# A Nyström attention fused with a feed-forward: all attention stages as tokens of one woven order

## The chip, the cores and the metric

The kernel runs on one core of one Trainium2 chip. The metric is the device time of one execution in microseconds (us). Engines are named as the profile does: PE is the matrix engine, PEld its weight loads, DVE the vector engine, ACT the activation engine, POOL the GpSimd engine and SP the engine that here only issues DMAs. PE, DVE, ACT and POOL each work through one instruction stream in order; so does each DMA-issuing queue (SP, ACT, POOL).

## The reference, cut to what matters

Batch 8, heads 8, sequence 576, head size 64, 32 landmarks. The output is `(A Z C v)` of each batch and head, laid out as tokens of 512 features, followed by a feed-forward.

```
q_lm, k_lm = means of 18 consecutive rows of q and of k          # 32 landmarks
A  = softmax(scale * q    k_lm^T)      # 576 x 32
Bm = softmax(scale * q_lm k_lm^T)      # 32 x 32
C  = softmax(scale * q_lm k^T)         # 32 x 576
Z  = Bm^T / (norm1(Bm) * norminf(Bm))
for _ in range(6): Z = 2 Z - Z Bm Z    # an approximate inverse
x  = (A Z C v)                         # rows of 512: heads side by side
out = (((x @ w1) * (x @ w2)) @ w3) @ w_out
```

## The kernel before, in words

**Folded weights.** `w3 @ w_out` is formed once (`fold`, L472), as 64 products of three matmuls each (L497) in split FP16, and kept as `w34`. Before it, tiles of w3 are transposed on PE (L484, "turn"), and both factors are split in a high and a low part by ACT and DVE (L477, L478, L489, L490). The products are a generator, and `steps(fd, n)` (L528) issues the next n of them, so that they fill PE while the first batch's attention is prepared.

**Attention of a batch.** The generator `attention` (L200) issues the stages of one batch, and each `yield` is a place where other work may be put in between. The eight heads are two quads of four heads. In order:

- scores C of a quad (`scores_c`, L205): twelve matmuls with 96 weight columns (a piece of transposed k), 64 moving columns each, into a `big` PSUM tile; an exp on ACT gives `ect` (L215). `presum` (L219) adds six parts of it on POOL to `es`, from which the column sums come.
- scores B, their exp and row sums, `bm` on POOL (L235 to L249); then its transposes and norms on DVE and POOL (L253 to L277).
- scores A (L283) with exp, and between the quads a product for the inverse's first residual (L303).
- context of a quad (`cv`, L313): 24 matmuls of C's exps with v (L317), followed by four small matmuls with a column of ones, one a head, for the sums (L322), a reciprocal and a scaled copy into `sz_`.
- six inverse steps (L376), each sixteen instructions on 32 x 32 array tiles, then two DVE evacuations (`tz_` L381, `sz_` L383) that the next step needs. Between them stand the row sums of A (`denominators`, L337), their reciprocals (L346) and the mix (L350, L352), which `normalise` (L357) spreads over partitions and multiplies into A.
- a closing product and `zt` (L398 to L404), then the product with the first-layer weights (L419), which gives `gt` ("widened" weights, evacuated by ACT L423 and DVE L425).

**Feed-forward of a batch.** `up` (L429) makes one 128-row piece of `x @ w1` or of `x @ w2` (named u and v below in the old order): four matmuls of 288 columns. The first kind is copied by ACT (L437), the second multiplied with it by DVE into `ab` (L439). There are 16 ups a batch. `down` (L446) multiplies 128 tokens of `ab` by `w34` in two halves of four matmuls with 512 columns (L451); after the second half ACT scales the sum into `o_sb` (L460), which is sent out.

**Loads.** q and k come in FP16 through POOL's queue; for batch 0 they are transposed on PE, for the others by DMA transposes on SP (`transposes`, L102; `turn_all` issues all four of a batch). `sums` (L171) adds the transposed rows to landmarks on POOL, with the DMA issues of a later batch's q and k in between; `landmarks` (L184) finishes them with a copy on ACT and an add on POOL. v comes in four pieces on SP, each after a one-element copy on ACT (L84).

**PSUM.** There are three `big` tiles (two banks each), one `small` and one `acc` tile.

**Order.** An opening (L548 to L624) loads weights, runs the fold and the attention of batch 0, in which the list of L605 says how many products go behind each attention step. The main loop (L646) then runs the ups of batch b while it steps through attention of batch b + 1. The order is a string of tokens, written out by hand, in which `a` is the next attention step:

```
MIXED = "u0 g a v0 u1 a v1 d u2 a v2 a d u3 v3 a s u4 v4 a p u5 d a v5 u6 a p v6 d a u7 p v7 a"
EVEN = "d a h p a h d a k d a d"
```

Of the kernel before, what the change touches and what calls it, by code (L numbers as in the profile page):

```python
# [31 lines left out]
def kernel(  # L32
# [11 lines left out]
    nc = tc.nc  # L44
    consts = ctx.enter_context(tc.tile_pool(name="consts", bufs=1))
# [55 lines left out]

    def transposes(st, t, hs):  # L102
        if "qkT" not in st:
            st["qkT"] = pat.tile([128, 2, H, 3, NP], FP16, name="qkT")
        n = len(hs)
        nc.sync.dma_start_transpose(
            out=st["qkT"][:, t, hs[0]:hs[0] + n, :, :].rearrange("p h c s -> p (h c) s"),
            in_=st["qkn"][0:NP, t, hs[0]:hs[0] + n, :].rearrange("p h f -> p (h f)"))


    def turn_on_pe(st, t, h0, copy):
        if "qkT" not in st:
            st["qkT"] = pat.tile([128, 2, H, 3, NP], FP16, name="qkT")
# [18 lines left out]
    def constants():  # L132
# [22 lines left out]
        nc.vector.memset(selc, 0.0)  # L155
        nc.vector.tensor_tensor(out=selr, in0=eye[:, 0, 0:8], in1=eye[:, 0, 8:16], op=ALU.add)
        nc.vector.reduce_sum(out=lomask, in_=eye[:, 0, 8:16], axis=AX.X)
        nc.vector.tensor_scalar(out=lomask, in0=lomask, scalar1=-1.0, scalar2=None, op0=ALU.mult)
        for c in range(4):
            sl = slice(32 * c, 32 * c + 32)  # L160
            for qd in range(2):
                nc.vector.tensor_copy(
# [4 lines left out]
        nc.vector.tensor_tensor(out=eye2, in0=eye, in1=eye, op=ALU.add)  # L167
# [32 lines left out]
    def attention(st, bank=None):  # L200
        bank = bank or small
        qkT, vt, qbd = st["qkT"], st["vt"], st["qbd"]
        ects = []

        def scores_c(qd):  # L205
            psC = big()
            pc = psC.rearrange("p a f -> p (a f)")
            for h in range(4):
                for c in range(3):
                    o = 64 * (3 * h + c)  # L210
                    nc.tensor.matmul(pc[0:NP, o:o + 64], qkT[:, 1, 4 * qd + h, c, :],  # L211
                                     qbd[:, 4 * qd + h, :, :].rearrange("p a m -> p (a m)"),
                                     start=True, stop=True)
            ect = pat.tile([128, 4, 6, 32], FP32, name="ect")
            nc.scalar.activation(out=ect[0:NP].rearrange("p h r m -> p (h r m)"),  # L215
                                 in_=pc[0:NP, 0:768], func=AXF.Exp, scale=SCALE / GRP)
            ects.append(ect)

        def presum(qd):  # L219
            e = ects[qd][0:NP]  # L220
# [3 lines left out]
            es = pz.tile([128, 4, 32], FP32, name="es")  # L224
# [3 lines left out]
            return es  # L228

        scores_c(0)  # L230
        es0 = presum(0)
        yield

        lm = st["lm"]
        psB = small()  # L235
        for qd in range(2):
            for h in range(4):
                nc.tensor.matmul(psB[32 * h:32 * h + 32, 32 * qd:32 * qd + 32],
                                 qbd[0:64, 4 * qd + h, 0, :], lm[0:64, 4 * qd + h, :],
                                 start=True, stop=True, tile_position=(0, 32 * h))  # L240
        ebm = pz.tile([128, 2, 32], FP32, name="ebm")
        nc.scalar.activation(out=ebm, in_=psB[:, 0:64].rearrange("p (a m) -> p a m", m=32),
                             func=AXF.Exp, scale=SCALE / (GRP * GRP))
        rbs = pz.tile([128, 2], FP32, name="rbs")
        nc.vector.reduce_sum(out=rbs, in_=ebm, axis=AX.X)
        nc.vector.reciprocal(out=rbs, in_=rbs)
        bm = pz.tile([128, 2, 32], FP32, name="bm")
        nc.gpsimd.tensor_tensor(out=bm, in0=ebm,
                                in1=rbs.unsqueeze(2).to_broadcast([128, 2, 32]), op=ALU.mult)  # L249
        yield  # L250

        scores_c(1)
        bt = pz.tile([128, 2, 32], FP32, name="bt")  # L253
        nc.vector.transpose(out=bt, in_=bm)
        btm = pz.tile([128, 2, 2, 32], FP32, name="btm")
        nc.gpsimd.tensor_tensor(
            out=btm, in0=bt.unsqueeze(2).to_broadcast([128, 2, 2, 32]),
            in1=par32.unsqueeze(1).unsqueeze(3).to_broadcast([128, 2, 2, 32]), op=ALU.mult)
        cs = pz.tile([128, 2], FP32, name="cs")
        nc.vector.reduce_sum(out=cs, in_=bt, axis=AX.X)  # L260
        es1 = presum(1)
        yield

        csT = pz.tile([128, 2, 32], FP32, name="csT")
        nc.vector.transpose(out=csT, in_=cs.unsqueeze(2).to_broadcast([128, 2, 32]))
        nrn = pz.tile([128, 2], FP32, name="nrn")
        nc.vector.reduce_max(out=nrn, in_=csT, axis=AX.X)
        nc.vector.tensor_scalar(out=nrn, in0=nrn, scalar1=-1.0, scalar2=-1e-6,
                                op0=ALU.mult, op1=ALU.add)
        nc.vector.reciprocal(out=nrn, in_=nrn)  # L270
        bmn = pz.tile([128, 2, 32], FP32, name="bmn")
        nc.gpsimd.tensor_tensor(out=bmn, in0=bm,
                                in1=nrn.unsqueeze(2).to_broadcast([128, 2, 32]), op=ALU.mult)
        bmbd = pz.tile([128, 2, 4, 32], FP32, name="bmbd")
        nc.gpsimd.tensor_tensor(
            out=bmbd, in0=bmn.unsqueeze(2).to_broadcast([128, 2, 4, 32]),
            in1=mask4.unsqueeze(1).to_broadcast([128, 2, 4, 32]), op=ALU.mult)  # L277
        yield


        eat = []

        def scores_a(qd):  # L283
            psA = big()
            for c in range(2):
                for h in range(4):
                    nc.tensor.matmul(
                        psA[32 * h:32 * h + 32, c, 0:HS],
                        lm[64 * c:64 * c + 64, 4 * qd + h, :],
# [38 lines left out]

        cv(1, es1, side())
        psX = small()  # L330
        cv(0, es0, psX)
        yield

        def denominators():
# [378 lines left out]
```

## Time and profile before

| what | value |
|---|---|
| median of 4 runs | 281.85 us (281.27 to 282.11) |
| profiled execution, its own time | 281.27 us |
| its span | 279.5 us |
| PE, PEld busy | 262.0 us, 150.1 us |
| DVE, ACT, POOL busy | 152.5, 143.2, 166.7 us |
| PE clock granted | 0.995 of full speed |
| HBM over the span | 173 GB/s |

The span is the time from the first to the last instruction on the core; the execution's own time also has what lies around it. A row of the profile's groups has the source line, the engine and operation, what it writes from what it reads, partitions by elements, how often, the busy time in us and the mean of one in ns, then the idle time of the engine just before such instructions and what ended most of it. Rows in order of time begin with the start and the length in us. Matmuls overlap in a pipeline and their ends are modelled, so what a stage costs is read from one start to the next.

### The profile page before, as it was taken

The page shows a single profiled execution, that of the slowest core. Times are in us where ns is not written, and L with a number is a line of the kernel's source. Part 1 is how long each engine was busy: PE and PEld are TensorE (multiplying, and loading weights), DVE is VectorE, ACT ScalarE, POOL GpSimd, SP SyncE. Part 2 cuts the span into 40 slices and gives each one's busy share as a digit, 9 for nine tenths or more (in the row PEclk, how much of TensorE's full clock was granted, in tenths as well). Part 3 has the DMA queues.
Part 4 walks back from the last instruction along what each step waited for, and adds up shares of the span by engine and source line. Part 5 has one row for each costly group of instructions (what it writes and reads, how often), then busy time and mean ns, then how long its engine had stood idle before and what let it go on. Part 6 is the DMA issues. An engine that isn't in the chain of part 4 may idle for free.

```text
span 279.5 us, 9468 instructions
## 1 busy us (share of the span) xinstructions
PE 262.0 (94%) x3964; PEld 150.1 (54%) x3964; DVE 152.5 (55%) x391; ACT 143.2 (51%) x275; POOL 166.7 (60%) x226
## 2 busy tenths in 40 slices
PE   7999999999989999999999999998998999999993
PEld 3556555444664575457536654664474456545641
DVE  7744123654468457645765475558565646665410
ACT  2644354225753863477456636654763467335531
POOL 1627872496599789848985994599589528100000
PEclk9999999999999999999999999999999999999998
DMA  6999999999919998989798999689995531112224
GB/s 207 321 237 259 226 260 170 193 252 131 145 45 193 182 149 172 228 192 167 139 239 172 167 156 242 139 168 167 217 172 110 165 90 47 26 40 75 77 75 113
DMA packets 61978, 45.57 MB, mean 163 GB/s; under 512 B 35568, under 2 KB 54000, under 8 KB 61936
## 3 DMA queue, kind: packets, MB, share of 16 engines
q1 hardware_dynamic: 47280, 31.93, 50.4%
q0 software_dynamic: 13824, 11.54, 28.1%
q10 hardware_dynamic: 832, 1.51, 1.6%
q8 instruction: 31, 0.51, 0.7%
q14 instruction: 11, 0.09, 0.1%
HBM read 38.80 MB, written 9.44 MB: 173 GB/s over the span
## 4 chain that ended last, share of the span: by engine, by line
PE 75%; ACT 9%; issue 5%; DVE 5%; POOL 4%; ACTq 0%; POOLq 0%; DVEq 0%
PE big L433 18%; PE acc L451 15%; PE acc L497 10%; PE big L451 6%; PE big L419 6%; ACT a_sb L437 5%; PE big L376 4%; ACT ect L215 2%; PE big L484 2%; DVE ab L439 2%; PE small L317 2%; PE big L565 2%; PE acc L317 2%; PE big L361 2%; PE big L211 2%
## 5 line engine op out<-in xcount | busy, mean ns | idle before, releaser
L433 PE MATMUL big<-ahat,gt 128*128 128x288 f16 x512 | 76.4, 286 | 4.9 <-ACT a_sb L437 2.8
L439 DVE TENSOR_TENSOR ab<-a_sb,big 128x576 f16<-128x576 f16 x64 | 48.0, 750 | 32.0 <-ACT a_sb L437 16.0
L433 PEld LDWEIGHTS <-gt 128*128 128x128 f16 x512 | 47.0, 98 | 23.7 <-issue 4.9
L437 ACT CAST a_sb<-big 128x576 f16<-128x576 f32 x64 | 40.7, 636 | 34.5 <-PE big L433 32.8
L451 PE MATMUL acc<-w,ab 128*128 128x512 f16 x216 | 55.1, 380 | 0.0
L497 PE MATMUL acc<-wsp,w3t 128*128 128x512 f16 x168 | 40.9, 379 | 0.8 <-ACT w L500 0.8
L451 PEld LDWEIGHTS <-ab 128*128 128x128 f16 x288 | 26.1, 98 | 28.2 <-issue 5.9
L176 POOL TENSOR_TENSOR tr<-qkT 128x768 f32<-128x768 f16 x16 | 26.2, 1639 | 7.8 <-DMA qkT<-qkn 7.6
L460 ACT ACTIVATE o_sb<-acc 128x512 f32<-128x512 f32 (+1 forms) x27 | 15.9, 589 | 28.3 <-PE acc L451 26.8
L196 POOL TENSOR_TENSOR lm<-o,far 64x256 f16<-64x256 f32 x16 | 11.5, 721 | 28.6 <-ACT far L195 28.4
L497 PEld LDWEIGHTS <-w3t 128*128 128x128 f16 x192 | 17.9, 98 | 19.5 <-issue 2.0
L425 DVE TENSOR_SCALAR gt<-big 128x1024 f16<-128x1024 f32 x16 | 19.6, 1224 | 15.7 <-PE big L419 15.7
L177 POOL TENSOR_TENSOR tr<-tr,qkT 128x768 f32<-128x768 f32 x16 | 26.2, 1640 | 1.3
L490 DVE SCALAR_TENSOR_TENSOR w3t<-big,w3t 128x512 f16<-128x512 f32 x16 | 11.0, 690 | 19.5 <-ACT w3t L489 19.4
L423 ACT ACTIVATE gt<-big 128x1024 f16<-128x1024 f32 x16 | 16.4, 1023 | 7.3 <-PE big L419 7.3
L222 POOL TENSOR_TENSOR t<-ect 96x384 f32<-96x384 f32 x16 | 15.9, 993 | 4.8 <-ACT ect L215 4.8
L451 PE MATMUL big<-w,ab 128*128 128x512 f16 x72 | 18.3, 381 | 0.0
L419 PE MATMUL big<-wup,zt 64*32 64x512 f16 x512 | 17.0, 379 | 0.0
L489 ACT ACTIVATE w3t<-big 128x512 f16<-128x512 f32 x16 | 9.5, 595 | 11.0 <-PE big L484 10.9
L196 POOL TENSOR_TENSOR qbd<-o,far 64x256 f16<-64x256 f32 x16 | 11.7, 729 | 4.6 <-ACT far L195 4.1
L215 ACT ACTIVATE ect<-big 96x768 f32<-96x768 f32 x16 | 12.9, 807 | 2.4 <-PE big L211 2.3
L181 POOL TENSOR_TENSOR o<-o,tr 128x256 f32<-128x256 f32 x16 | 12.8, 801 | 1.3
(313 smaller groups left out, 365.3 us busy)
## 6 DMA issues: line engine op xcount, KB each, us to landing
vt<-in_v_dram SPq DMA_DIRECT2D x28, 288.0 KB, 5.0
out_dram<-o_sb SPq DMA_DIRECT2D x23, 192.0 KB, 2.4
qkn<-in_q_dram POOLq DMA_DIRECT2D x12, 288.0 KB, 5.9
qkn<-in_k_dram POOLq DMA_DIRECT2D x12, 288.0 KB, 6.6
w3f<-in_moe_w_dram SPq DMA_DIRECT2D x6, 512.0 KB, 7.4
out_dram<-o_sb SPq DMA_DIRECT2D x24, 128.0 KB, 2.5
wup<-in_moe_w_dram POOLq DMA_DIRECT2D x4, 512.0 KB, 32.0
out_dram<-o_sb SPq DMA_DIRECT2D x24, 64.0 KB, 3.3
```

The source lines that it names most:

```text
L176: nc.gpsimd.tensor_tensor(out=tr, in0=x[:, :, 0, :], in1=x[:, :, 1, :], op=ALU.add)
L177: nc.gpsimd.tensor_tensor(out=tr, in0=tr, in1=x[:, :, 2, :], op=ALU.add)
L196: nc.gpsimd.tensor_tensor(out=st["lm"][own] if t else st["qbd"][own, :, parity, :], in0=o[own], in1=far[own], op=ALU.add)
L215: nc.scalar.activation(out=ect[0:NP].rearrange("p h r m -> p (h r m)"), in_=pc[0:NP, 0:768], func=AXF.Exp, scale=SCALE / GRP)
L419: nc.tensor.matmul(psG[32 * h:32 * h + 32, qd, :], zt[rs, i, h, :], wup[rs, h, w, fs], start=(i == 0), stop=(i == 1), tile_position=(64 * ...
L423: nc.scalar.activation(out=g[:, :, w, fs], in_=psG, func=AXF.Copy, scale=1.0 / ZS)
L425: nc.vector.tensor_scalar(out=g[:, :, w, fs], in0=psG, scalar1=1.0 / ZS, scalar2=None, op0=ALU.mult)
L433: nc.tensor.matmul(p[:, c, 0:HS], st["g"][:, qd, w, 128 * j:128 * j + 128], st["ahat"][qd][:, c, :], start=(qd == 0), stop=(qd == 1))
L437: nc.scalar.copy(out=st["a_sb"], in_=p[:, :, 0:HS])
L439: nc.vector.tensor_tensor(out=st["ab"][:, j, st["t0"]:st["t0"] + S].rearrange("p (c s) -> p c s", c=2), in0=st["a_sb"], in1=p[:, :, 0:HS], ...
L451: nc.tensor.matmul(pso[:, :], ab[:, j, t0:t0 + 128], w34[:, j, :], start=(j == 0), stop=(j == 7))
L497: nc.tensor.matmul(psW[j][:, :], turned[j, c // 4][:, a, c % 4, :], wsp[:, b, c, :], start=(c == 0 and a + b == 0), stop=(c == 7 and a == 1))
```

## The change: what it does

- Each attention stage is a function of its own, and a dictionary maps a letter to each. The order of everything, opening included, is now in token strings. `START` replaces the list of L605, and `FIRST`, `EVEN`, `ODD` and `LAST` replace the old strings. A token takes the next batch for which that stage hasn't run. f is a fold product, u the next up, d or db a half of a down (into `acc` or `big`), s one `sums`, h one `landmarks`, t one DMA transpose, p one piece of v, w the last w3 load.
- Scores C of a batch are issued near the end of the batch before the one in which the rest of its attention stands. Four of the 64 fold products, and no transposes of w3, move from the opening into `FIRST`.
- C's matmuls take 128 weight columns in place of 96, from a flat view of the transposed k, so that 32 columns of the next piece come along; the exp still reads 96 partitions. Only the last piece of a batch has 96.
- The four matmuls with 32 weight columns for a quad's sums become one with 128, and stand before the context, as a token (S) of their own.
- B, the residual, the context and the sums of a batch share one `small` tile.
- A dummy activation of one column, whose value is not used, stands after the first two DMA issues of ACT's queue. One load of w_out moves from ACT's queue to SP's.
- Part of the constants (`selc`, `selr`, `eye2`) are made on POOL in place of DVE, and all constants stand ahead of POOL's gate and of the first q/k loads.
- The last transpose of w3 comes one product earlier. `wsp` and `w3t` lie in a pool of their own, and the two `ab` buffers in two pools.

```
+    START = ("C0 h f f f f h S0 B w f C1 f V0 T N P f f f S1 A1 A0 V1 R f s p f D f f s f I0 "
+             "J0 p f I1 f p I2 f J2 J1 f I3 f f f X p I4 f I5 f M1 M0 Z f h f f t G0 G1 h G2 "
+             "G3 f t t f h h C0 t C1 f f ")
+    FIRST = ("u u p u S0 u B p u p u T V0 N P A1 f S1 A0 u R u u u s V1 u D s J0 I0 f f I1 "
+             "J1 u I2 J2 u u I3 X f I4 M0 I5 h u u h d M1 Z d G0 G1 h C0 t p h t t d C1 G2 "
+             "G3 t db ")
+    EVEN = ("p u u d p u S0 u B p A1 u V0 T u N db S1 u u u P R u A0 V1 s u s I0 D J0 J1 d "
+            "t I1 u I2 u J2 I3 X u d I4 p M0 t u I5 u Z h d G0 h G1 db db t h h db C0 M1 C1 "
+            "G2 G3 t ")
+    ODD = ("u S0 p u B T u p N V0 p d A1 R u u S1 u u d u A0 V1 P u s I0 u D s J0 I1 u d "
+           "J2 I2 u I3 J1 u u I4 db u X I5 u M0 h d p Z h t M1 d db db C0 G0 t h t G1 G2 d "
+           "h t G3 d C1 ")
+    LAST = ("u u u u u db d u u u d u u u u u u u d u db db d db db db db db db db ")
...
+                    w0 = NP * (3 * (H + 4 * qd + h) + c)
+                    n = min(128, 2 * H * 3 * NP - w0)
+                    nc.tensor.matmul(pc[0:n, o:o + 64], st["flat"][:, w0:w0 + n],
+                                     st["qbd"][:, 4 * qd + h, :, :].rearrange("p a m -> p (a m)"),
                                      start=True, stop=True)
...
-            for h in range(4):
-                nc.tensor.matmul(psV[32 * h:32 * h + 32, 64:65], es[0:NP, h, :], ones[0:NP, :],
-                                 start=True, stop=True, tile_position=(0, 32 * h))
...
+        def sums_c(qd):
+            if qd == 0:
+                f["psX"] = small()
+                f["sz"] = pz.tile([128, 2, 96], FP32, name="sz0")
+            psV = f["psX"][:, 66 * qd:66 * qd + 65]
+            nc.tensor.matmul(psV[:, 64:65], ess[qd][0:NP, :, :].rearrange("p h m -> p (h m)"),
+                             ones[0:NP, :], start=True, stop=True)
+            rcr = f["rcr", qd] = pz.tile([128, 1], FP32, name="rcr")
             nc.vector.reciprocal(out=rcr, in_=psV[:, 64:65])
...
+        return dict(B=rows_b, T=turned_b, N=norms, P=scaled_b, R=residual, D=denominators, X=mixed,
+                    Z=closing, C=scores_c, A=scores_a, V=context, S=sums_c, J=inverted, M=normalise,
+                    I=inverse, G=lambda i: widened(i // 2, i % 2))
...
-            before[8 * j] = [(turn, j, 1)]
+            before[8 * j - (j == 7)] = [(turn, j, 1)]
...
+    def all_sums():
+        for b in range(1, B):
+            pieces = qk_pieces(sts[b + 1], b + 1) if b + 1 < B else iter(())
+            for t in (0, 1):
+                sums(sts[b], t, pieces=pieces)
+                yield
...
+    queues = dict(p=loads_v(), s=all_sums(), h=all_landmarks(), t=all_turns(), u=all_ups())
+
+    def run(names):
+        for t in names.split():
+            if t[0] in queues:
+                next(queues[t[0]], None)
+            elif t == "f":
+                steps(fd)
+            elif t == "w":
+                load_w3(7)
+            elif t[0] == "d":
+                piece(acc if t == "d" else lambda: big()[:, 0, :])
+            else:
+                n = done[t] = done.get(t, -1) + 1
+                while len(atts) <= n and n < B:
+                    atts.append(attention(sts[len(atts)]))
+                if n < B:
+                    atts[n][t[0]](*([int(t[1])] if t[1:] else []))
...
+        warm = pf.tile([128, 512], FP16, name="warm", bufs=1)
+        nc.vector.memset(warm, 0.0)
         load_w3(0, 0)
         load_wout(0, nc.scalar)
         load_wout(1, nc.sync)
         load_w3(1, 0, nc.scalar)
         load_wout(2, nc.sync)
+        nc.scalar.activation(out=gate, in_=warm[:, 0:1], func=AXF.Copy, scale=1.0)
         load_wout(3, nc.scalar)
         load_w3(0, 1)
         load_wout(4, nc.scalar)
         load_w3(1, 1)
-        load_wout(5, nc.scalar)
...
+        load_wout(5, nc.sync)
...
+        par32, mask4, ones, eye2, onesq, selc, lomask = constants()
         nc.gpsimd.tensor_copy(out=gate, in_=wof[4][:, 0:1])
         load_qk(sts[0], 0)
         load_qk(sts[1], 1)
```

## The prediction

> **What bounds the kernel now.** I read the page's busy shares first, then the stretches of one batch each, then the order of time of TensorE (PE) alone, because PE is the engine that hardly rests.
>
> ```profile
> PE 262.0 (94%) x3964; PEld 150.1 (54%) x3964; DVE 152.5 (55%) x391; ACT 143.2 (51%) x275; POOL 166.7 (60%) x226
> ...
> 8.00:70.60 62.60, 60.67 (x654) 32.41 (x653) 26.78 (x57) 26.98 (x52) 38.49 (x49) 1.00 1.16 224
> 70.60:94.30 23.70, 21.65 (x438) 13.23 (x437) 15.39 (x40) 13.92 (x28) 20.45 (x27) 1.00 0.75 137
> 94.30:121.40 27.10, 26.29 (x461) 15.30 (x460) 16.18 (x41) 15.55 (x31) 20.68 (x28) 1.00 0.99 188
> 121.40:147.00 25.60, 24.52 (x453) 14.60 (x452) 16.21 (x41) 15.05 (x30) 20.56 (x27) 1.00 0.93 178
> ```
>
> The stretches (columns: PE, PE weight loads, DVE, ACT, POOL, clock, DMA share, GB/s) are the opening with attention of batch 0, then batches 0, 1 and 2 of the main loop. PE fills each at a full clock, and POOL is second with 20.6 of 25.6 us. But a busy PE is not one that streams, so I lay batch 2 out by the starts of its pieces:
>
> ```profile
> 121.90 0.69 PE L211 MATMUL big<-qbd,qkT 128*96 128x64 f16 x12
> 122.42 1.14 PE L433 MATMUL big<-ahat,gt 128*128 128x288 f16 x8
> 123.49 0.22 PE L238 MATMUL small<-lm,qbd 64*32 64x32 f16 x8
> 124.09 0.65 PE L433 MATMUL big<-ahat,gt 128*128 128x288 f16 x4 [0.38 <-ACT ect L215]
> ...
> 135.57 0.40 PE L376 MATMUL big<-sz__2457,tz__2455 32*32 32x96 f32 x16
> 136.37 0.65 PE L433 MATMUL big<-ahat,gt 128*128 128x288 f16 x4 [0.40 <-ACT a_sb L437]
> ...
> 142.23 1.03 PE L451 MATMUL acc<-w,ab 128*128 128x512 f16 x4
> 143.18 1.06 PE L419 MATMUL big<-wup,zt 64*32 64x512 f16 x32
> ```
>
> From start to start: an up (u) takes 0.49 us, half a down (d) 0.864, a fold product (f) 0.648, a pair of widened tiles 0.99, scores C 0.52 a quad, scores B 0.25, scores A with the residual 0.60, context and sums of both quads 1.58, an inverse step 0.33, denominators 0.24, a normalise 0.25, the closing 0.38. Entering a narrower array tile costs 0.09 (142.23 + 0.864 = 143.09, next start 143.18), eleven times a batch, 1.1 with some spread. A batch without waits is 16 u (7.84) + 8.49 of attention + 1.1 = 17.43, plus 0.864 a d. Batches 0 to 6 have 4, 10, 8, 10, 8, 10, 8 d and last 23.69, 27.13, 25.61, 27.73, 25.62, 28.29, 25.63 us from first u to first u; their waits are 2.8, 1.1, 1.3, 1.7, 1.3, 2.2, 1.3, together 11.6. From 8.0 to 70.59 the work is 64 f (41.5), 14 weight turns (6.0), two q/k turns (2.0), attention 9.6 = 59.1 of 62.6: 3.4 of wait. So about 15 us of the path are waits that an order can change; the rest is array work.
>
> **The change, part by part.** (1) C with 128 weight columns.
>
> ```profile
> L211 PEld LDWEIGHTS <-qkT 128*96 128x96 f16 x192 | 10.9, 125 | 1.5 <-issue 0.8
> L451 PEld LDWEIGHTS <-ab 128*128 128x128 f16 x288 | 26.1, 98 | 28.2 <-issue 5.9
> L322 PEld LDWEIGHTS small<-ones,es 96*32 96x32 f32 x64 | 1.6, 110 | 1.1 <-issue 1.1
> L484 PE MATMUL big<-ident,w3f 128*128 128x128 f32 x64 | 10.3, 286 | 0.0
> L222 POOL TENSOR_TENSOR t<-ect 96x384 f32<-96x384 f32 x16 | 15.9, 993 | 4.8 <-ACT ect L215 4.8
> ```
>
> A load of 96 columns lasts 125 ns, the wider one 98. Twelve C matmuls take 0.52 us, 43 ns each; by the matmul rows 288 columns cost 122 ns and 512 cost 216, so 64 should cost 29. Loads bind here, and with quick ones a quad is 0.35: -0.17 x 16 = -2.7 at most, 0 at least. The Trainium skill (TensorE: Matmul & The Clock Gate, "Weight-path perf modes — Fast Weight Load (FWL) and DoubleRow") says that the quick load needs exactly 128 weights of a type other than FP32, which fits; but its "LDWEIGHTS (loading the stationary operand)" gives columns/1.2 ns, 80 ns for 96, from which C would lose 0.61 x 16 = 9.8 us. The measured 43 ns excludes that. I take -2.2, near the upper bound, since the first load of each burst stays.
>
> (2) Column sums: eight narrow instructions a quad (four matmuls, two passes each in FP32) become two with 128 columns. Now both quads cost 0.21 a batch. The nearest row, L484 (FP32, 128 columns), runs four in 0.43, 0.108 each, so 0.22 a quad: +0.11 x 16 = +1.8; with nothing of its load hidden it is 0.141 each (+2.8), with all of it under the neighbouring u it is a small gain (-0.5). I take +1.0.
>
> (3) The weave. START, FIRST, EVEN and ODD hold 12, 14, 13 and 13 groups that enter a narrow tile from the full array, against 11 each now: 1 + 3 + 6 x 2 = 16 more. "Key Properties" of TensorEngine Tiling (Array Packing) says that a change of mode drains the engine; that speaks against this change. The row has 0.09 an entry, up to 0.15 with the exit: +1.4 to +2.4; I take +1.6.
>
> (4) Waits. The 0.38 or 0.18 behind scores B goes, since C is now issued a batch ahead and its exp no longer holds a `big` buffer in front of a u. Batch 0 loses most: its inverse steps have too little between them (0.57, 0.58 and 0.40 waited), and four f's (2.6 us, taken out of the opening) come in. A chain step needs 1.07 us (L376 at 53.12 to L376 at 54.22, with one f between); where only one u stands between two steps the PE has 0.33 + 0.09 + 0.49 = 0.91, so 0.15 is late next, more where an `ab` multiply (0.75) goes first on DVE. EVEN ends in C0 M1 C1 G2 G3, five `big` tiles for three buffers: G2 waits for C0's exp behind an output copy (0.4), C1 for a down's tile (0.2). By this walk the opening goes from 3.4 to 1.5, batch 0 from 2.8 to 0.8, ODD (1, 3, 5) from 4.9 together to 2.4, EVEN (2, 4, 6) stays at 3.9: 15.0 to 8.6, -6.4. Ends: -13 (2 us left in all) and +12 (the second rival).
>
> (5) The start.
>
> ```profile
> 5.12 1.28 ACT L477 ACT_TABLE_LOAD   x1 [5.12 <-DMA w3f<-in_moe_w_dram]
> ...
> 6.60 0.23 PEld L484 LDWEIGHTS big<-ident,w3f 128*128 128x128 f32 x1 [0.28 <-DMA w3f<-in_moe_w_dram]
> ```
>
> The dummy moves 1.28 us of table load under the first loads. But PE reaches its first product (7.99) only after the turn at 7.03, which waits for a transfer and not for ACT; so little is on the path. The dummy also stands ahead of two DMA issues on ACT's queue, w_out 3 and 4, and piece 4 opens POOL's gate (7.8 us waited, until 9.43) ahead of the q/k loads; k was waited for 2.2 us at 22.3. Ends -1.0 and +0.9; I take -0.3. The constants on POOL (12 small operations, some 3 us by their DVE rows of 0.2 to 0.5) lie in that wait; without it they delay the q/k loads one for one.
>
> (6) At nothing. Turns go to SP one by one. In EVEN the first stands 2 PE-us after a `sums` that issues its source (q 5.9, k 6.6 us to landing), so SP is held for about 6 us with one output and one v load behind it; three `o_sb` buffers and v's use a batch later hide that; without them a d would wait. v's marks cost ACT 0.19 each wherever they stand. The split `ab` pools free their space long before use. LAST is 16 u and 14 d (19.9 us) as before.
>
> Sum: -2.2 + 1.0 + 1.6 - 6.4 - 0.3 = -6.3. The profiled execution took 281.27 (span 279.5, 1.8 around it), 0.58 under the median of the four, 281.85; so 275.0 for its like and 275.5 for the median.
>
> **The rivals.** First, the waits keep their size: a three-buffer `big` ring and one-u gaps give back what the weave takes. For it: my walk of EVEN finds no gain. Against: batch 0 and the opening have clear holes. Then -6.4 becomes about 0 and the time is 281.9, 279 to 284.
>
> Second, POOL becomes the bound, and the kernel slower. POOL works in order:
>
> ```profile
> 130.97 1.64 POOL L176 TENSOR_TENSOR tr<-qkT 128x768 f32<-128x768 f16 x1
> ...
> 142.61 0.69 POOL L93 DMA_DIRECT2D qkn<-in_k_dram  x1
> 143.32 1.54 POOL L196 TENSOR_TENSOR qbd<-o,far 64x256 f16<-64x256 f32 x2
> ```
>
> Two `sums` with their DMA issues hold it for 12.3 us, and landmarks, es (0.99 + 0.45 + 0.45) and bm queue behind. S0 of the next batch needs es: 3.0 us after C0's matmuls (exp 0.81, 1.89, hand-offs), while from C0 to S0 the PE has M1 C1 G2 G3 u, 2.2 us. Each us that POOL is late stops PE six times; over 1.15 us a batch the sum turns slower. At 2 us it is 12 - 6.3: 287.5. Against: now POOL idles 5 us of 25.6, and bm is used only some u's later.
>
> Third, nearly all waits go (2 us left) and nothing else is worse than taken: 275.5 - 6.6 = 268.9. That the wide C load is not quicker is a rival inside the first case: 277.7.
>
> **How the numbers follow.** The forecast 0.47 (272.5 to 278.5), third rival 0.13, both faster. First rival 0.25: 0.10 faster, 0.05 within 0.2%, 0.10 slower. Second 0.15, slower. So 0.70, 0.05, 0.25; 0.2% (0.56 us) is about what a measurement of this kernel can tell from no change. The range 268 to 286 takes in the third rival and the first and half of the second.
>
> **What would show it.** Right: L211's weight load near 98 ns and twelve in under 0.4 us; sums as 32 instructions; batches of 24 to 27.5 us; first u at 66 to 67 us (70.59 less four f, 1.9 of waits and 0.3 each for the start and C, plus C of batch 1); no wait of a u on ect. Wrong: PE waiting for `es` or `bm` behind `tr`; PE waiting on `big` at G2; q/k landing later than 22.3.

## The result and the profile after

The changed kernel takes 280.78 us (median of 43 executions, 278.87 to 285.16), the kernel before 282.28 in the same sessions (64 executions). The ratio is 0.9934, 95% interval 0.9917 to 0.9951: 1.9 us faster, where the prediction said 6.3. The ratio leaves out the slow executions (so it differs from that of the two medians), and the profiles of after, e3_s4 and e5_join fell on such ones, which shows in their openings; from the first up of batch 0 to that of batch 7, the stretch compared below, every profile here has the clock at 1.00. All lines of after below are from a second profile of the same kernel (span 278.6 us against 279.5 before); in the loop, from that first up on, it agrees with the first profile to 0.01 us a batch.

The page's busy shares, and then the stretches from 7.40 us to the first up and of batches 0, 1 and 2 (columns as in the prediction):

```profile
PE 263.8 (95%) x3868; PEld 147.8 (53%) x3868; DVE 151.6 (54%) x380; ACT 144.2 (52%) x276; POOL 171.1 (61%) x237
...
7.40:69.10 61.70, 58.81 (x654) 32.14 (x653) 27.21 (x56) 28.62 (x54) 39.55 (x51) 1.00 1.13 226
69.10:94.70 25.60, 24.56 (x438) 14.22 (x437) 15.64 (x40) 13.65 (x29) 21.16 (x29) 1.00 0.96 150
94.70:121.80 27.10, 26.68 (x449) 14.94 (x448) 16.50 (x41) 15.27 (x32) 21.28 (x29) 1.00 1.01 178
121.80:147.60 25.80, 24.94 (x447) 14.42 (x444) 15.15 (x40) 15.50 (x32) 20.04 (x26) 1.00 0.96 189
```

These rows hardly differ from before: batches of 25.6, 27.1 and 25.8 us against 23.7, 27.1 and 25.6, and batch 0 now has four fold products (2.6 us) that the opening had. Busy shares can't tell where 4 us of the forecast went. The order of time on PE can; this is the end of batch 2 and part of batch 3, an ODD batch:

```profile
146.60 1.06 PE L412 MATMUL big<-wup,zt 64*32 64x512 f16 x32 [0.17 <-ACT ect L233]
147.59 0.66 PE L429 MATMUL big<-ahat,gt 128*128 128x288 f16 x4
148.81 0.38 PE L334 MATMUL small<-ones,es 96*128 96x1 f32 x2 [0.55 <-POOL es L242]
149.05 0.65 PE L429 MATMUL big<-ahat,gt 128*128 128x288 f16 x4
149.63 0.22 PE L249 MATMUL small<-lm,qbd 64*32 64x32 f16 x8
149.78 0.66 PE L429 MATMUL big<-ahat,gt 128*128 128x288 f16 x4
150.38 0.88 PE L322 MATMUL small<-vt,ect 96*32 96x64 f32 x48
151.19 1.04 PE L447 MATMUL acc<-w,ab 128*128 128x512 f16 x4
...
153.52 0.28 PE L334 MATMUL small<-ones,es 96*128 96x1 f32 x2
153.66 1.14 PE L429 MATMUL big<-ahat,gt 128*128 128x288 f16 x8
...
174.73 0.53 PE L229 MATMUL big<-qbd,qkT 128*128 128x64 f16 x12
175.10 1.14 PE L429 MATMUL big<-ahat,gt 128*128 128x288 f16 x8
```

The contexts of batch 2 before:

```profile
129.48 0.88 PE L317 MATMUL acc<-vt,ect 96*32 96x64 f32 x48
...
130.23 0.86 PE L317 MATMUL small<-vt,ect 96*32 96x64 f32 x48
...
131.06 1.15 PE L433 MATMUL big<-ahat,gt 128*128 128x288 f16 x8
```

Three readings. C takes 174.73 to 175.10, 0.37 (0.35 elsewhere), where it took 0.52. S standing alone takes 0.14 (153.52 to 153.66) and pays no entry: it starts 0.49, one up, behind the up before it. V standing alone takes 0.81 from its first product to the next up or down, and 0.11 passes before it starts (149.78 + 0.49 = 150.27); joined, V and S of both quads took 1.58 (129.48 to 131.06), 0.79 a quad with the way out. And there is a new wait: S0 stands still for 0.55 us because `es`, POOL's sum of C's exps, isn't there.

The same lay-out for all batches, with the prediction's piece times and the three corrections just read (per batch: C -0.34; the two V alone +0.22, the two S +0.10, two more entries +0.18, together +0.50), gives work and wait. A wait here is what is left of a stretch when the work is taken off:

| from first up to first up | before: length, waits | after: length, waits | waits forecast |
|---|---|---|---|
| batch 0 | 23.69, 2.8 | 25.59, 1.9 | -2.0 |
| ODD 1, 3, 5 | 27.13, 27.73, 28.30; 4.9 together | 27.12, 27.51, 27.50; 3.5 | -2.5 |
| EVEN 2, 4, 6 | 25.61, 25.62, 25.63; 3.9 | 25.78, 25.77, 24.65; 3.4 | 0 |
| opening, first product to first up | 62.60, 3.5 | 61.55, 4.2 | -1.9 |

(Batch 6 has no C after. The opening's work is 59.1 before and about 57.3 after: four products less, 2.6; two more C, two quicker ones, and the standing apart of S and V, together +0.8.) From the first up of batch 7 to the end it takes 25.6 after and 25.2 before.

The idle times in brackets, summed, would mislead here. Over the loop they fall from 8.4 to 3.7 us, about what was forecast, and yet the loop is 0.2 longer: a short wait has no bracket at all. In batch 2 of after two inverse steps stand with one up between, and from an up to a step 0.58 is usual (0.49 and an entry); here it is 0.80 and 0.92, and only the second shows:

```profile
133.99 0.67 PE L429 MATMUL big<-ahat,gt 128*128 128x288 f16 x4
134.79 0.40 PE L378 MATMUL big<-sz,tz 32*32 32x96 f32 x16
135.13 0.66 PE L429 MATMUL big<-ahat,gt 128*128 128x288 f16 x4
136.05 0.40 PE L378 MATMUL big<-sz,tz 32*32 32x96 f32 x16 [0.26 <-DVE sz L385]
```

### The profile page after: what moved, and what is told of

The parts are those of the page before. It is cut to its first block, busy times and chain, and to the rows that moved or that the text cites. A ratio compares the mean times of both kernels' runs of the same rounds, so it can differ in the third digit from the quotient of the medians.

```text
span 283.4 us, 9334 instructions
## 1 busy us (share of the span) xinstructions
PE 263.7 (93%) x3868; PEld 147.5 (52%) x3868; DVE 151.5 (53%) x380; ACT 144.3 (51%) x276; POOL 171.2 (60%) x237
## 4 chain that ended last, share of the span: by engine, by line
PE 59%; DMA 15%; POOL 9%; DVE 5%; SPq 4%; ACT 4%; issue 2%; POOLq 0%; DVEq 0%
PE big L429 20%; PE acc L447 15%; PE big L447 7%; DMA qkn<-in_q_dram 6%; DMA qkT<-qkn 5%; SPq L123 4%; PE big L378 4%; PE small L322 4%; DMA wof<-in_moe_w_out_dram 3%; PE big L412 3%; POOL t L237 1%; DVE ab L435 1%; POOL tr L193 1%; POOL tr L194 1%; DVE sz L385 1%
## 5 line engine op out<-in xcount | busy, mean ns | idle before, releaser
L429 PE MATMUL big<-ahat,gt 128*128 128x288 f16 x512 | 78.6, 287 | 0.7 <-DVE ahat L366 0.6
L429 PEld LDWEIGHTS <-gt 128*128 128x128 f16 x512 | 45.3, 100 | 19.9 <-issue 2.5
L447 PE MATMUL acc<-w,ab 128*128 128x512 f16 x200 | 51.4, 380 | 0.0
L493 PE MATMUL acc<-wsp,w3t 128*128 128x512 f16 x168 | 41.6, 380 | 3.1 <-issue 1.6
L456 ACT ACTIVATE o_sb<-acc 128x512 f32<-128x512 f32 x25 | 14.9, 597 | 17.4 <-PE acc L447 14.6
L378 PE MATMUL big<-sz,tz 32*32 32x96 f32 (+1 forms) x768 | 18.6, 248 | 2.3 <-DVE sz L385 1.3
L447 PE MATMUL big<-w,ab 128*128 128x512 f16 x88 | 20.5, 379 | 0.0
L412 PE MATMUL big<-wup,zt 64*32 64x512 f16 x512 | 17.6, 379 | 0.9 <-ACT ect L233 0.5
L378 PEld LDWEIGHTS big<-sz,tz 32*32 32x32 f32 x768 | 9.1, 103 | 16.9 <-issue 12.7
L383 DVE TENSOR_TENSOR tz<-big,eye 128x64 f32<-128x64 f32 x40 | 8.8, 220 | 16.0 <-PE big L378 15.9
L485 ACT ACTIVATE w3t<-big 128x512 f16<-128x512 f32 x16 | 9.5, 597 | 14.7 <-PE big L480 14.6
L366 DVE TENSOR_TENSOR ahat<-eat,big 128x576 f16<-128x576 f16 x16 | 11.9, 749 | 6.6 <-PE big L363 6.6
```

What stands on the lines that cost most here:

```text
L378: nc.tensor.matmul(psI[32 * t:32 * t + 32, qd, o:96], tz[sl, qd, :], sz[sl, qd, o:96], start=True, stop=True, tile_position=(32 * h, 32 * t))
L412: nc.tensor.matmul(psG[32 * h:32 * h + 32, qd, :], zt[rs, i, h, :], wup[rs, h, w, fs], start=(i == 0), stop=(i == 1), tile_position=(64 * ...
L429: nc.tensor.matmul(p[:, c, 0:HS], st["g"][:, qd, w, 128 * j:128 * j + 128], st["ahat"][qd][:, c, :], start=(qd == 0), stop=(qd == 1))
L447: nc.tensor.matmul(pso[:, :], ab[:, j, t0:t0 + 128], w34[:, j, :], start=(j == 0), stop=(j == 7))
L493: nc.tensor.matmul(psW[j][:, :], turned[j, c // 4][:, a, c % 4, :], wsp[:, b, c, :], start=(c == 0 and a + b == 0), stop=(c == 7 and a == 1))
```

## The experiments

A ratio below is to the kernel before, timed beside each on the same chip. The first seven but e1_after edit the changed kernel, and "the loop" is the stretch from the first up of batch 0 to that of batch 7.

**e1_after**, the changed kernel itself, unedited.

> The changed kernel again, for a profile to set beside the first one and a closer ratio. Theory A (the opening is bound by a chain of transfers: q/k of batch 1, their DMA transposes, sums and landmarks on POOL, then scores C of batch 1, which now stand ahead of the first up): the first up starts where qkT of batch 1 lands plus about 16 us, in every profile, and the two profiles differ by the same amount at the landing and at the first up; from the first up on they agree within 0.5 us. Theory B (the loop's waits vary): the first ups agree and the loop differs. Ratio to the kernel before 0.991 to 0.996 by both.

Measured: 280.52 us, ratio 0.9944 (0.9920 to 0.9969). This is the profile shown above. The first up is at 69.10, the third of POOL's `tr` sums (the first of batch 1) starts at 53.12, and 15.98 us lie between them. In the longer first profile the two are 73.84 and 57.87, 15.97 apart. It is 15.97 to 16.04 in seven of the traces, these two among them, while the third `tr` itself moves between 52.9 and 57.9.

**e2_c96**, C with 96 columns again:

```
-                    n = min(128, 2 * H * 3 * NP - w0)
+                    n = NP
```

> The changed kernel with 96 weight columns in scores C again, all else kept. If the wide weight load saves its 0.17 us a quad on the path (0.35 from start to start against 0.52), 14 quads outside the opening's waits make it 2.4 us slower than the changed kernel (1.5 to 2.7). If C's time is covered by other waits (PSUM tiles behind the exp), under 0.7 us.

Measured: 281.68, ratio 0.9957 (0.9932 to 0.9981). The interval overlaps that of e1_after, so the times give no verdict. The traces do: the loop takes 184.32 us with 96 columns and 183.93 with 128. Twelve C of 0.17 us are 2.0 us of work; 0.4 of that is seen. One place where the rest went: the wait for `ect` at G2, 0.17 above, isn't listed in the trace with 96 columns.

**e3_s4**, the sums as four narrow matmuls a quad, at their new place:

```
-            nc.tensor.matmul(psV[:, 64:65], ess[qd][0:NP, :, :].rearrange("p h m -> p (h m)"),
-                             ones[0:NP, :], start=True, stop=True)
+            for h in range(4):
+                nc.tensor.matmul(psV[32 * h:32 * h + 32, 64:65], ess[qd][0:NP, h, :], ones[0:NP, :],
+                                 start=True, stop=True, tile_position=(0, 32 * h))
```

> The changed kernel with four narrow column-sum matmuls a quad in place of one full one, at the same place between full-array matmuls. If the full one is the dearer by its FP32 weight load (two of 190 ns), this is 1 us faster. If standing alone is what costs, the narrow ones here have to enter the narrow tile each time (0.09 and a way out): 1 to 2 us slower than the changed kernel.

Measured: 282.36, ratio 0.9976 (0.9953 to 1.0000), which overlaps e1_after's; the loop is 185.13, 1.2 us longer than in after, about 14 entries of 0.09. So the full-width sum belongs to the weave: for a product that stands alone between two ups it is right, though its loads (190 ns) are longer than the narrow ones (108 ns in this trace). The groups of the two weight loads in after's profile, C's and the sums':

```profile
L229 PEld LDWEIGHTS <-qkT 128*128 128x128 f16 x184 | 7.3, 98 | 4.0 <-issue 1.3
L334 PEld LDWEIGHTS small<-ones,es 96*128 96x128 f32 x32 | 5.4, 190 | 3.1 <-POOL es L242 2.1
```

**e4_c_later**, C of batch 1 moved from the end of START into FIRST, so that the first up need not wait for it:

```
-             "G3 f t t f h h C0 t C1 f f ")
-    FIRST = ("u u p u S0 u B p u p u T V0 ...
+             "G3 f t t f h h t f f ")
+    FIRST = ("u C0 u p u C1 u S0 p u B p u T V0 ...
```

> The changed kernel with only scores C of batch 1 moved from the end of START to behind the first and the third up of FIRST, where they stood before the change. Theory A: the first up no longer stands behind the chain of transfers; it starts some 1.5 us or more earlier and the kernel is 1 to 2.5 us faster. Theory B, or if the rest of START is as long: the work is only moved, within 0.5 us of the changed kernel; slower by up to 1 us if the es of C then holds up S0.

Measured: 282.08, ratio 0.9979 (0.9955 to 1.0003). The tie is undone: in its trace the third `tr` starts late, at 56.05, and the first up at 69.60, only 13.55 later; with 16 us between them it would have stood at 72. But batch 0 grows from 25.59 to 27.84. Two C moved in are 0.7 of that, and one row shows half:

```profile
73.88 0.38 PE L333 MATMUL small<-ones,es 96*128 96x1 f32 x2 [1.18 <-POOL es L241]
```

The C that is late makes S0 wait for `es`. What the opening saves against the tie, 2.4, batch 0 pays with 2.3.

**e5_join**, contexts, residual and scores A side by side again in FIRST, EVEN and ODD:

```
-            "p u u d p u S0 u B p A1 u V0 T u N db S1 u u u P R u A0 V1 s u s I0 D J0 J1 d t I1 ...
+            "p u u d p u S0 u B p u T u N db S1 u u u P u A1 R A0 V0 V1 s u s I0 D J0 J1 d t I1 ...
```

> The kernel after, with FIRST, EVEN and ODD alone rewritten so that scores A of the second quad, the residual, scores A of the first quad and both contexts stand side by side (A1 R A0 V0 V1) in place of five places between ups. Work and stages are the same. Theory 1 (each separate place costs its own entry into narrow tiles and unhidden first loads, about 0.3 to 0.45 us a batch): the seven batches are shorter by 2 to 3 us together, median near 278. Theory 2 (what is lost is waits behind the vector and scalar engines, and separate places cover them): the joined stages wait for one another's exps and PSUM space, the batches keep their length or grow, median 280.5 or up to 283.

Measured: 288.03, ratio 1.0228 (1.0157 to 1.0298). Theory 1 falls: the loop takes 191.75 us in place of 183.93. Batch 3 of its trace shows where:

```profile
160.98 0.65 PE L426 MATMUL big<-ahat,gt 128*128 128x288 f16 x4 [0.60 <-DVE ab L432]
...
164.03 0.88 PE L319 MATMUL small<-vt,ect 96*32 96x64 f32 x48 [0.56 <-DVE sz L310]
165.34 0.88 PE L319 MATMUL small<-vt,ect 96*32 96x64 f32 x48 [0.43 <-ACT sz L323]
```

The second V waits for the copy of the first one's result (`sz`), since all of B, R, V and S now write one `small` tile; and the ups that stood between the stages now stand together and wait for the multiply that frees their PSUM. Before, the quads' contexts lay in `acc` and `small` and could stand side by side at no wait. So within the one-tile layout the standing apart, which I charged at +0.09 an entry, pays: it costs 0.50 us of PE a batch, and without it the batches are 1.1 us longer. (The edit also puts V0 and scores A later in the batch; how much of the 1.1 that makes, no run shows.)

**e6_wup_later**, the four loads of w_up issued some 5 us later on POOL's queue:

```
-        load_weight(0, moe_w1)
-        load_weight(1, moe_w2)
...
         load_w3(4)
+        load_weight(0, moe_w1)
+        load_weight(1, moe_w2)
```

> The kernel after, with the four loads of w_up (512 KB each, on POOL's queue) issued behind the load of w3's column 4, some 5 us later, so that q and k of batch 1 share the wire with less. Theory A (the opening is bound by the chain q/k of batch 1, DMA transposes, three sums and landmarks on POOL, C of batch 1, first up): the third sum starts at 51 to 52.5 us in place of 53.1, the first up follows it by 16 us until PE's own work is the bound near 68.9; median 0.5 to 1.5 us lower than after's, and less spread between executions. Rival (only PE's own order sets the opening): first up unchanged at 69.1, median 280.5.

Measured: 280.34, ratio 0.9942 (0.9908 to 0.9977). The loads are issued at 20.2 in place of 14.7; the third `tr` at 53.07 and the first up at 69.10 are those of after: w_up doesn't hold the transposes.

**e7_old_start**, the start of before: no dummy, `load_wout(5)` on ACT's queue, constants on DVE and behind the gate:

```
-        nc.scalar.activation(out=gate, in_=warm[:, 0:1], func=AXF.Copy, scale=1.0)
...
-        load_wout(5, nc.sync)
+        load_wout(5, nc.scalar)
...
-        par32, mask4, ones, eye2, onesq, selc, lomask = constants()
         nc.gpsimd.tensor_copy(out=gate, in_=wof[4][:, 0:1])
...
+        par32, mask4, ones, eye2, onesq, selc, lomask = constants()
```

> The kernel after, with the start of before: no dummy activation, the load of w_out 5 on the scalar engine's queue, all constants on the vector engine and behind POOL's gate. If the new start delays the q/k loads by about 1 us and the opening hangs on them: POOL's gate opens near 9.4 us in place of 10.5 to 10.9, the third sum starts about 1 us earlier, the first product is 0.6 us later (8.0), the first up 68.5 to 69 and the median 0 to 1 us lower. If the dummy's early table load is what pays: first up 0.6 us later, median 281.1.

Measured: 280.41 (279.88 to 281.42), ratio 0.9924 (0.9892 to 0.9957). POOL's gate, in after's trace and in this one:

```profile
10.87 0.19 POOL L635 COPY gate<-wof 128x1 f32<-128x1 f32 x1 [3.62 <-DMA wof<-in_moe_w_out_dram]
```

```profile
9.41 0.66 POOL L633 COPY gate<-wof 128x1 f32<-128x1 f32 x1 [7.76 <-DMA wof<-in_moe_w_out_dram]
...
52.03 1.64 POOL L193 TENSOR_TENSOR tr<-qkT 128x768 f32<-128x768 f16 x1 [5.93 <-DMA qkT<-qkn]
```

The new start opens the gate 1.5 us later (in all traces it ends at 10.6 to 11.1 with the new start, 9.1 to 10.1 with the old), and in this pair the third `tr` comes 1.1 later (53.12); with the old start alone it lies between 52.0 and 54.7, so one pair doesn't tell how much of that the gate makes. The first up is at 68.74 against 69.10, though the chain gave 1.1 (16.71 us now lie between the third `tr` and the first up, not 15.98): here PE's own work sets it.

The first product stands at 7.43 here and at 7.55 in after, but over all fourteen traces at 7.4 on the mean with the new start and 7.8 with the old: some 0.4 is gained there. It doesn't last. Behind 28 us stands the same product in before, then in after:

```profile
28.89 3.40 PE L497 MATMUL acc<-wsp,w3t 128*128 128x512 f16 x15 [0.29 <-ACT w L500]
```

```profile
28.92 3.40 PE L493 MATMUL acc<-wsp,w3t 128*128 128x512 f16 x15 [0.81 <-ACT w L496]
```

It waits for ACT's copy of a finished row of `w34` out of `acc`, which stands on ACT behind a landmark copy that needs POOL's first sums; these start when k of batch 0 has landed (22.41 and 22.44). From that first `tr` to this product it takes 6.48 to 6.54 us in ten of the fourteen traces. So a quicker start of PE is waited away by 28.9 us. The medians, 280.41 here and 280.34 in e6_wup_later on the same chip, show no worth of the new start either way.

**e8_before_c128**, the kernel before with nothing but the 128 columns of C:

> The kernel before, with scores C on 128 weight columns from the flat view and nothing else changed. If C's loads lie on PE's path there: 16 quads by 0.17 us, 2.2 to 2.7 us faster than before, median near 279.7, and the twelve matmuls start to start 0.35 us in place of 0.52. If C is covered by the exp and by PSUM space that the next up waits for: 0 to 0.8 us faster, the wait of the next up on ect longer by as much as C is shorter (0.38 to about 0.55).

```
-                    nc.tensor.matmul(pc[0:NP, o:o + 64], qkT[:, 1, 4 * qd + h, c, :],
+                    w0 = NP * (3 * (H + 4 * qd + h) + c)
+                    n = min(128, 2 * H * 3 * NP - w0)
+                    nc.tensor.matmul(pc[0:n, o:o + 64], st["flat"][:, w0:w0 + n],
```

Measured: 282.30, ratio 0.9974 (0.9934 to 1.0014). The loop takes 183.74 us; in the kernel before it takes 183.70. That the sums agree is in part chance. Of the two C of batches 1 to 6, the first is 0.17 to 0.19 shorter, and the ups behind it wait longer by as much; the second is 0.16 shorter, and nothing behind it answers that. Batches 2, 4 and 6 are 0.16 shorter each (25.46). But batches 3 and 5 have stalls put down to "issue" that are 0.42 and 0.32 longer than before, and in batch 1 half a down takes 0.25 more; no wait for C accounts for these. The group of the ups in the profile of before, then in this one; the number behind the bar's second half is PE's idle time before them:

```profile
L433 PE MATMUL big<-ahat,gt 128*128 128x288 f16 x512 | 76.4, 286 | 4.9 <-ACT a_sb L437 2.8 <-ACT ect L215 2.0
```

```profile
L435 PE MATMUL big<-ahat,gt 128*128 128x288 f16 x512 | 76.7, 286 | 6.0 <-ACT ect L217 2.9 <-ACT a_sb L439 2.8 <-DVE ab L441 0.2
```

The ups wait 0.9 us more for `ect` (2.0 to 2.9), and 1.1 more in all: C is quicker, and PE meets the exp sooner. By these rows about half of the 2.4 us that fourteen quicker C save in the loop is answered by waits.

The last four build on e7_old_start.

**e9_c0_early**, one token of EVEN:

```
-            "... G1 db db t h h db C0 M1 C1 "
+            "... G1 db db t h h C0 db M1 C1 "
```

> The kernel of e7_old_start with one token moved: in EVEN, C0 stands one half of a down (0.86 us) earlier, ahead of the last db in place of behind it. If S0's wait on es at the start of batches 3, 5 and 7's attention (0.55 us each) lies on PE's path, as its row says: that wait goes to zero, batches 3 and 5 last 27.0 us in place of 27.5 and batch 1 stays, median 1.0 to 1.6 us under e7_old_start's 280.4. If PE only meets its next wait sooner (an ab multiply, the third big buffer behind M1 and C1): batches stay within 0.15 us and the median at 280.4.

Measured: 279.52, ratio 0.9908 (0.9874 to 0.9942). The interval overlaps that of e7_old_start (0.9892 to 0.9957), but the batches speak plainly, and the loop takes 183.25 us in place of 184.02: batches 3 and 5 last 27.04 and 27.01 in place of 27.51, batches 2 and 4 25.89 and 25.91 in place of 25.78. Its trace around the turn from EVEN to ODD:

```profile
146.26 0.51 PE L229 MATMUL big<-qbd,qkT 128*128 128x64 f16 x12 [0.30 <-POOL qbd L213]
146.61 1.03 PE L447 MATMUL big<-w,ab 128*128 128x512 f16 x4
...
149.31 0.66 PE L429 MATMUL big<-ahat,gt 128*128 128x288 f16 x4
150.06 0.38 PE L334 MATMUL small<-ones,es 96*128 96x1 f32 x2
```

S0 starts 0.26 behind the up (149.31 + 0.49 = 149.80) in place of 0.73, and no wait for `es` is listed; the earlier C0 now waits 0.30 for its own input from POOL. The wait on `es` was on the path, and 0.1 of the 0.5 came back as another.

**e10_f_back**, batch 0's four fold products put back in the opening:

```
-             "G3 f t t f h h C0 t C1 f f ")
+             "G3 f t t f h h C0 t C1 f f f f f f ")
...     (and the four f of FIRST left out)
```

> The kernel of e7_old_start with the four fold products of batch 0 put back to the end of the opening; the order is otherwise the same. The prediction took 2.0 us off batch 0's waits by these products. If that is right: the opening is 2.6 us longer, batch 0 only 0.6 shorter (25.0), the median 2.0 us higher. If the products cover little there: opening 2.6 longer, batch 0 2.0 to 2.6 shorter, median within 0.6 us.

Measured: 282.03, ratio 1.0001 (0.9968 to 1.0033): 1.6 us over e7_old_start by the medians, 1.1 by the spans of the two traces (279.4 and 278.3). Batch 0 is only 0.74 shorter (24.91 against 25.65) for 2.6 us less of work:

```profile
81.61 0.40 PE L378 MATMUL big<-sz,tz 32*32 32x96 f32 x16 [0.74 <-DVE sz L385]
...
85.73 0.40 PE L378 MATMUL big<-sz,tz 32*32 32x96 f32 x16 [1.10 <-DVE sz L385]
...
92.22 0.51 PE L229 MATMUL big<-qbd,qkT 128*128 128x64 f16 x12 [0.49 <-POOL qbd L213]
```

So these products cover 1.9 us of waits, as much as the prediction took. But without them FIRST waits 3.8 us, where the order before waited 2.8: the new order of batch 0 is by itself 1 us worse, and the products first pay for that.

**e11_best**, e9_c0_early with three more tokens moved:

```
-"... A1 A0 V1 R f s p f D ..."               +"... A1 A0 V1 f R s p f D ..."
-"... I3 X f I4 M0 I5 h u u h d M1 ..."       +"... I3 X f u I4 M0 u I5 h h d M1 ..."
-LAST = ("u u u u u db d ..."                 +LAST = ("u u u u u d db ..."
```

> The kernel of e9_c0_early with three more tokens moved, each at a wait that the trace shows: in START a fold product between V1 and R (0.68 us waited for a copy of sz, as all stages of a batch share one small PSUM tile), in FIRST two ups put between the mix, I4, M0 and I5 (0.35 and 0.18 waited for sz), in LAST the first down's half into acc before the one into big (0.4 waited). If each wait was on PE's path and nothing else is late: 0.6 + 0.5 + 0.4 = 1.5 us under e9_c0_early. If they only move to the next dependence: 0 to 0.5.

Measured: 279.02, ratio 0.9876 (0.9832 to 0.9919), span 277.1: the lowest median of all, 1.2% under the kernel before, though its interval overlaps e9_c0_early's. The waits aimed at in START and FIRST are gone, and these stand in their places:

```profile
66.91 0.88 PE L229 MATMUL big<-qbd,qkT 128*128 128x64 f16 x24 [0.91 <-POOL qbd L213]
90.58 0.51 PE L229 MATMUL big<-qbd,qkT 128*128 128x64 f16 x12 [0.44 <-POOL qbd L213]
```

With 0.68 of wait taken out of the opening, C of batch 1 waits 0.91 for POOL's `qbd`: the first up stays at 68.91. Batch 0 gets 0.45 shorter. In LAST nothing changes (25.6 us to the end): the first down still starts 0.4 late, but the time is lost ahead of it. The second and third up, at 252.22 and 252.90, stand 0.71 and 0.68 behind the one before in place of 0.49, each just behind the end of a copy out of a `big` tile:

```profile
251.14 1.02 ACT L416 ACTIVATE gt<-big 128x1024 f16<-128x1024 f32 x1 [0.24 <-PE big L412]
```

```profile
251.65 1.22 DVE L418 TENSOR_SCALAR gt<-big 128x1024 f16<-128x1024 f32 x1 [0.34 <-PE big L412]
```

These are the third and fourth of batch 7's `gt`, which those ups don't read; so what they wait for is most likely the three `big` buffers.

**e12_turn_first**, e11_best with the DMA transposes of batch 1 ahead of the load of w3's column 6, which goes to POOL's queue:

```
-        load_w3(6)
         turn_all(1)
+        load_w3(6, eng=nc.gpsimd)
```

> The kernel of e11_best with the DMA transposes of batch 1 issued ahead of the load of w3's column 6 on SP's queue, and that load moved to POOL's queue. In e11_best SP reaches the first transpose only at 29.0 us, behind that load's wait for a buffer, and C of batch 1 waits 0.91 us for qbd at the end of the opening. If the w3 load holds the transposes: the third sum starts 1 to 3 us earlier (50 to 52 us in place of 52.9), C's wait goes, first up at 68.0 in place of 68.9, median 0.5 to 0.9 us lower. If the landing of q and k of batch 1 or the transposes' own rate holds them: third sum at 52.9 and first up at 68.9 as before; if the load of column 6 now comes late behind POOL's sums, PE waits for it and the first up is later.

Measured: 281.98, ratio 0.9977 (0.9938 to 1.0015). SP reaches the first transpose at 26.47 in place of 29.00, and still the third `tr` starts at 53.10:

```profile
26.47 26.81 SPq L123 DMA_TRANSPOSE qkT<-qkn  x4
```

The waits of SP's queue between 20 and 55 us tell what holds them. One is for the transposes (us in total, times, longest):

```profile
SPq L123 <- DMA qkn<-in_q_dram: 3.5, 1, 3.5
```

So the first transpose now waits for the landing of q; behind it SP waits for nothing that the trace lists, and the four follow one another for 26.8 us. k isn't what holds them: had SP waited for it, a row would say so. What is left is the transposes' own pace beside the other transfers. Meanwhile the load that was moved comes late:

```profile
52.08 0.63 PE L480 MATMUL big<-ident,w3f 128*128 128x128 f32 x4 [2.17 <-DMA w3f<-in_moe_w_dram]
```

The first up is at 71.08, 2.2 later than in e11_best. Batch 3 of this trace is 1.1 longer besides, with a stall of 0.80 put down to "issue" at an inverse step, which no edit accounts for.

## Why the prediction fell short

The sign, the pieces and the range held (280.8 lies in 268 to 286); the size did not. By its own steps:

**(1) C, -2.2: the mechanism right, the credit wrong.** The weight load is 98 ns and a quad 0.35 us, as forecast, and the quick load that the Trainium skill promises for exactly 128 weights ("Weight-path perf modes — Fast Weight Load (FWL) and DoubleRow" in TensorE: Matmul & The Clock Gate) is in the rows. But in e8_before_c128, which puts it alone into the kernel before, the batches without a stall are 0.16 shorter, not 0.34; in the new order 0.4 of 2.0 us is seen. Behind C stands an exp that frees PSUM for what comes next, and where PE waits for that exp, a quicker C only waits longer. The prediction had the row that says so (0.38 waited for `ect` two ups behind C) and counted it under another step.

**(2) and (3), the sums and the entries, +2.6: about +3.8.** S at 0.14 is within the ends given. The entries cost 0.09 to 0.11, as forecast. Missing was the cost of V standing alone (0.22 a batch). That the joined quads share an entry, an exit and first loads would explain it; no run takes these apart. By the ledger it is +0.50 a batch for S, V and entries, seven times, and 0.3 in the opening.

**(4) The waits, -6.4: the step that failed.** It took the listed waits off and counted too few that come in their places. The lay-outs give -2.8 in the loop, +0.7 in the opening and +0.4 behind the last batch's first up: -1.7. (In this ledger C's 0.17 counts as work saved, -2.7 in all, and what answers it as a wait that stayed. With +3.8 for (2) and (3) and a first product 0.4 earlier the sum is -1.0; the two spans differ by 0.9.)
- The opening (-1.9 forecast) gained nothing. Three waits at inverse steps went (0.80 together). In their places came, in rows of after: R behind V1's copy, since both write the shared `small` tile (0.68); 0.52 more at the product of 28.9 us; a G (0.28), a load of w3 (0.18), and `qbd` for C of batch 1 (0.18). And since that C now stands ahead of the first up, the opening also hangs on the transposes of batch 1 and POOL's sums. The trace of before has the third `tr` at 52.95 and the first up 17.6 us later; in after they are 16 apart, and whatever delays the transposes delays all. Two of the rows:

```profile
44.82 0.33 PE L308 MATMUL small<-bt,btm 64*32 64x32 f32 x16 [0.68 <-ACT sz L326]
...
67.09 0.88 PE L229 MATMUL big<-qbd,qkT 128*128 128x64 f16 x24 [0.18 <-POOL qbd L213]
```

- Batch 0 (-2.0 forecast) gained 0.9: the products do cover 1.9 (e10_f_back), and the order around them gave 1 back.
- ODD (-2.5 forecast) gained 1.4, and on the whole the order has no part in it: before has two stalls that its trace puts down to "issue", by the starts 0.6 in batch 3 and 1.1 in batch 5, and the prediction had counted both among the 4.9. In after's loop there is none, for a reason that no run shows. This is the longer one:

```profile
210.97 0.24 PE L322 MATMUL small<-ones,es 96*32 96x1 f32 x8 [0.96 <-issue]
```

The wait on `ect` went, and S0's wait on `es` came: the same exp, met one stage later. The prediction saw this, 3.0 us of chain against 2.2 of cover, and put it under its second rival only; it belonged in the forecast, at 0.55 twice (batches 3 and 5; e9_c0_early moves one token and 0.49 goes).
- EVEN (0 forecast) is right: batches 2 and 4 wait 1.3 as before, at the places that the walk named, one-up gaps, G2 (0.17, not 0.4) and C1. The 0.4 less is batch 6, which has no C behind it.

**(5) The start, -0.3: nothing.** Both ends named are real: the first product comes some 0.4 earlier, and the gate is late (10.87 in place of 9.43). The first is waited away by 28.9 us; the second is covered by PE's own work in e7_old_start's trace.

**The rivals.** The first, waits that keep their size, at 281.9, is nearer to 280.8 than the forecast. Of its two reasons, one-up gaps show in EVEN (0.80 and 0.92 in place of 0.58) and the ring of `big` buffers at G2 and most likely in LAST; the shared `small` tile it didn't name. The second, POOL as the bound, is right in its place (S0 behind `es`) and wrong in its cause: POOL stood idle for the exp before that sum, so the chain is long, not POOL full.

```profile
146.69 1.01 POOL L237 TENSOR_TENSOR t<-ect 96x384 f32<-96x384 f32 x1 [0.44 <-ACT ect L233]
```

**The signs named.** Load of 98 ns, 32 instructions of sums, batches of 24 to 27.5, no up waiting for `ect`: all there. First up at 66 to 67: 69.1, the sign that told of the failure. Of the signs of being wrong, two came: PE waited for `es`, though not behind `tr`, and on `big` at G2. k of batch 0 landed at 22.3 as before.

That the sign is right is in part luck, as far as these two traces go: of the 2.8 us of waits that the loop lost, 1.7 are the two stalls, which the weave wasn't meant to remove.

## What to carry to other kernels

When stages are put apart to cover waits, take each wait that goes and ask which later consumer of the same producer now stands in front of it; here the exp of C lost the waiting up and gained a waiting sum. A cheaper instruction is a gain only if the time to the next instruction that waits for its result can shrink too: lay the saving against the row behind it. And putting one stage of the next batch ahead of the loop ties the opening to that batch's whole chain of loads.

## What the runs showed of the hardware

- A weight load of 96 FP16 columns lasts 125 ns, of 128 columns 98; twelve C matmuls take 0.52 and 0.35 us start to start. The time of the kernel followed in part only.
- Weights in FP32 with 96 rows and 128 columns load in 190 ns (L334), narrow ones with 32 columns in 108 to 110; nevertheless, where the sums stand alone, two wide loads a quad were better than eight narrow ones, by 1.2 us over the loop.
- Four DMA transposes of batch 1 keep SP for 23.4 to 27.0 us from the first issue, and starting 2.5 us earlier didn't bring the first sum behind them forward (53.10 against 52.91).
